# Two groups of heads side by side in a gated recurrence with a two-layer block behind it

## The chip, the cores and the metric

The kernel runs on one core of a Trainium2 chip. The metric is the device time of one execution in microseconds, taken over several runs of the same program. The engines are named as in the profile: PE multiplies matrices (PEld loads its weights), DVE and ACT and POOL work on vectors, SP only issues transfers. Each engine takes its instructions in the order in which they stand in its own queue and waits on semaphores for the others.

## What is computed

For each of 4 x 8 heads a 40 x 40 state runs through 768 time steps. The output of a step is read from the state as it was before the step.

```python
for t in range(S):
    y[:, :, t] = np.einsum('bhd,bhde->bhe', rt, state)
    Sa = np.einsum('bhde,bhe->bhd', state, at)
    state_decay = state * wt[:, :, None, :] - np.einsum('bhd,bhe->bhde', Sa, bt)
    state = state_decay + np.einsum('bhd,bhe->bhde', vt, kt)
...
x = y.transpose(0, 2, 1, 3).reshape(B * S, H * D)      # 3072 x 320
h = x @ w_in                                           # 320 x 2048
sp = np.maximum(h, 0.0) + np.log1p(np.exp(-np.abs(h)))
out = (h * erf(sp)) @ w_out                            # 2048 x 320
```

## The kernel before

**Tiling.** The 32 heads form 2 groups of 16. Time is cut into 6 segments of 128 steps, and a segment into 4 chunks of 32. So there are 2 x 6 = 12 segment steps (`q`) and 48 chunks. In a chunk the recurrence becomes products of small matrices; only the state, held in `MT` for one group, goes from a chunk to the next.

**Per segment step.** `prep` loads the decays `w` into a tile of the ring `Pr` and scans them forward and backward on DVE. `aphase`, once for each chunk, loads `k`, `b` and `a` (`kba`, into `bk`), scales them (`ab`, `bk`), multiplies them on PE (`A`, line 677) into the scores, masks them into a tile of the ring `Zs`, copies that tile's rows by transfers (`zs`, `AD`) and keeps the transposed keys in the ring `sg` (`bT`, line 695). `tphase` inverts the triangular score matrices of the four chunks: transfers `Ti`, `Ap`, 28 short DVE operations (`Tm`, `Ts`), transfers `TD` and `tb`, and two rounds of products on PE (`W` and `DAD`, line 740). The inverses lie in the ring `Tb`.

**The chain.** `chain`, once for each chunk, is the part that is serial: copy the state to `Zm` (`zmm`), `Z` on PE (line 785), copy `zt`, `U` on PE (line 794) with the inverse, copy `us`, from there four transfers `zu` into `Vu` and a transpose `UT` (line 821), copy `vtu`, `PQ` (line 830), mask `PQm`, and `MY` (lines 841 and 845), which gives the output of the chunk and the increment of the state. `MT` (line 848) adds it to the state, `Ym` (line 852) puts the output aside. `pmt` (line 812) transposes the state for `MY`. `v` and `r` come by the transfers `zv`, `vx`, `rt`, `rv`.

**The two-layer block.** When the four chunks of a segment are done, their 256 rows go to DRAM (`xw`) and come back transposed (`xr`, in `load_x`). `mm1` (line 1006, 192 in all, 8 matmuls each) makes `h`; `tanh`, `unit` and `post` form `h * erf(sp)` on ACT, DVE and POOL (`nd` line 1038, `rho` line 1039, `E` line 1050, `G` line 1051); `mm2` (line 1060) multiplies by `w_out`. At the start, `weights` turns both weight matrices from float64 to float32 with DVE, ACT and POOL work (`w1` to `w6`), after transfers `wd`.

**The order.** Every operation is recorded with its inputs, outputs and a priority. The instructions are then written out in the order of the table `ORDER`, on the engine that the string `ENGINES` names for each (P, A, V, G for POOL, S for SP). An entry -1 or -2 in `ORDER` is a filler: a 128x512 matmul on PE whose result nobody reads (`warm`, line 579). All transfers go through the helper `dma` (line 576), which issues on the engine that `ENGINES` names, SP or POOL. Here 493 transfers are recorded for SP and 414 for POOL, which also does 85 operations of vector work. All 24 chunks of group 0 come before those of group 1, and `mlp(q)` follows the chain of step `q`. The rings have 8 tiles `Zs`, 8 `sg`, 3 `Pr`, 2 `Tb`, 2 `Vu`, 2 `Rt`, 2 `vt` and 1 each of `Zm`, `Us`, `Sm` and `zt`; there is one state `MT`.

Of the kernel before, what the change touches and what calls it, by code (L numbers as in the profile page):

```python
# [1198 lines left out]
```

## Time and profile before

| | |
|---|---|
| median of 3 runs | 826.29 us (821.66, 826.29, 826.45) |
| profiled execution | 821.56 us, its span 819.8 us, so 1.8 us lie around the span |
| mean granted TensorE clock | 0.974 |
| busy in the span | PE 728.6, PEld 567.6, DVE 635.4, ACT 568.8, POOL 352.8 us |
| transfers | 98.98 MB, 49.95 MB in the queue of SP and 46.88 MB in that of POOL |

Busy time is an average over a start in which PE mostly waits, a long middle and an end. A row of the list of groups gives line, engine, operation, output and inputs, shapes and count; behind the first bar the busy time and the mean duration of one in ns; behind the second the idle time of the engine just before and what ended most of it. A row of the timeline gives start and duration in us. Where several matmuls stand in one row, their durations overlap, so the row's length and not the mean is what PE spent.

### The profile page before, as it was taken

The page shows a single profiled execution, that of the slowest core. Times are in us where ns is not written, and L with a number is a line of the kernel's source. Part 1 is how long each engine was busy: PE and PEld are TensorE (multiplying, and loading weights), DVE is VectorE, ACT ScalarE, POOL GpSimd, SP SyncE. Part 2 cuts the span into 40 slices and gives each one's busy share as a digit, 9 for nine tenths or more (in the row PEclk, how much of TensorE's full clock was granted, in tenths as well). Part 3 has the DMA queues.
Part 4 walks back from the last instruction along what each step waited for, and adds up shares of the span by engine and source line. Part 5 has one row for each costly group of instructions (what it writes and reads, how often), then busy time and mean ns, then how long its engine had stood idle before and what let it go on. Part 6 is the DMA issues. An engine that isn't in the chain of part 4 may idle for free.

```text
span 819.8 us, 32461 instructions
## 1 busy us (share of the span) xinstructions
PE 728.6 (89%) x13753; PEld 567.6 (69%) x13753; DVE 635.4 (78%) x1343; ACT 568.8 (69%) x1077; POOL 352.8 (43%) x503
## 2 busy tenths in 40 slices
...
GB/s 248 207 219 113 184 118 148 131 118 131 118 134 107 129 118 146 134 159 128 132 93 136 138 121 122 133 110 123 136 133 119 121 102 76 98 43 54 12 17 20
DMA packets 128728, 98.98 MB, mean 121 GB/s; under 512 B 88112, under 2 KB 111264, under 8 KB 128576
## 3 DMA queue, kind: packets, MB, share of 16 engines
q1 hardware_dynamic: 108144, 49.95, 25.5%
q0 software_dynamic: 20432, 46.88, 21.7%
q8 instruction: 110, 1.80, 0.9%
...
HBM read 75.07 MB, written 14.16 MB: 109 GB/s over the span
## 4 chain that ended last, share of the span: by engine, by line
PE 48%; DMA 15%; DVE 13%; ACT 10%; issue 8%; POOL 3%; SPq 2%; DVEq 0%; POOLq 0%; ACTq 0%
PE po L1060 17%; PE ph L1006 12%; DMA Vu<-Us 3%; PE pA L740 3%; PE my L841 3%; ACT r L1014 3%; ACT l L1014 2%; PE pA L677 2%; DMA Tb<-TD 2%; PE my L785 2%; PE my L794 2%; SPq L576 2%; DMA wo<-in_moe_w_in 2%; PE pQ L812 2%; PE pQ L830 2%
## 5 line engine op out<-in xcount | busy, mean ns | idle before, releaser
L1060 PE MATMUL po<-wo,h 128*128 128x320 f32 x768 | 250.7, 455 | 6.1 <-DVE h L1051 5.3
L1060 PEld LDWEIGHTS po<-wo,h 128*128 128x128 f32 x768 | 136.7, 195 | 49.0 <-DVE h L1051 7.0
L1014 ACT ACTIVATE l<-l 128x512 f32<-128x512 f32 x192 | 111.9, 626 | 10.7 <-DVE nd L1038 9.8
L576 POOL DMA_DIRECT2D Vu<-Us x88 | 49.5, 567 | 115.1 <-ACT Us L571 76.1
L1006 PE MATMUL ph<-xh,wih 128*128 128x256 f32 x384 | 97.5, 335 | 0.8 <-ACT h L571 0.8
L1006 PE MATMUL ph<-xl,wih 128*128 128x256 f32 x384 | 77.3, 283 | 0.0
L1006 PE MATMUL ph<-xh,wil 128*128 128x256 f32 x384 | 77.2, 283 | 0.0
L1051 DVE SCALAR_TENSOR_TENSOR h<-l,h 128x512 f32<-128x512 f32 x96 | 71.3, 748 | 2.2 <-POOL l L1050 1.4
L1039 DVE SCALAR_TENSOR_TENSOR r<-nd,r 128x512 f32<-128x512 f32 x96 | 67.9, 707 | 4.6 <-POOL nd L1038 2.8
L1006 PEld LDWEIGHTS ph<-xh,wih 128*128 128x128 f32 x384 | 61.9, 190 | 11.9 <-ACT h L571 1.6
L1038 DVE TENSOR_TENSOR nd<-l,r 128x512 f32<-128x512 f32 x80 | 57.4, 718 | 14.3 <-ACT r L1014 11.2
L841 PE MATMUL my<-Vu,sg 64*40 64x72 f32 x1536 | 49.4, 232 | 14.3 <-DMA Vu<-Us 5.2
L571 ACT COPY Zm<-MT 40x320 f32<-40x320 f32 x66 | 30.1, 456 | 45.0 <-DVE MT L848 41.8
L1006 PEld LDWEIGHTS ph<-xh,wil 128*128 128x128 f32 x384 | 59.8, 191 | 0.0
L1006 PEld LDWEIGHTS ph<-xl,wih 128*128 128x128 f32 x384 | 59.5, 191 | 0.0
L1014 ACT ACTIVATE l<-h 128x512 f32<-128x512 f32 x96 | 56.3, 627 | 3.9 <-DVE h L573 2.1
L571 ACT COPY h<-ph 128x512 f32<-128x512 f32 x82 | 47.1, 584 | 16.7 <-PE ph L1006 12.4
L579 PE MATMUL ph<-d 104*128 104x512 bf16 x216 | 57.5, 416 | 0.0
L841 PEld LDWEIGHTS my<-Vu,sg 64*40 64x40 f32 x1536 | 37.3, 115 | 28.3 <-issue 6.0
L1014 ACT ACTIVATE r<-r 128x512 f32<-128x512 f32 x96 | 55.0, 623 | 0.3
L1050 DVE TENSOR_TENSOR l<-l,r 128x512 f32<-128x512 f32 x75 | 52.1, 701 | 3.2 <-ACT l L1014 2.6
L1014 ACT ACTIVATE r<-l 128x512 f32<-128x512 f32 x96 | 54.5, 619 | 0.0
...
## 6 DMA issues: line engine op xcount, KB each, us to landing
...
```

Of the source, the lines that this page charges most:

```text
L571: self.nc.scalar.copy(o, i)
L576: self.P.add(name, "SP", lambda e: self.eng(e).dma_start(o(), i()), rd, wr, pr, ISSUE.get(name, 0.41))
L579: self.nc.tensor.matmul((self.ph[1], self.pQ)[x], self.d1[:, :128], self.d1[:, :512], start=True, stop=True)
L740: nc.tensor.matmul(pw[js, i], l[js, i], r[js, i], start=True, stop=True)
L841: nc.tensor.matmul(my[h * 64:h * 64 + 40, x, j], sg[xs, j, h], vu[xs, j // 2 * 2 + h, j % 2], start=True, stop=False)
L1006: nc.tensor.matmul(ph[:, j * 256:j * 256 + 256], a[:k, fs], b[:k], start=(m == 0), stop=(m == 7))
L1014: self.P.add(name, "ACT", lambda e: nc.scalar.activation(out=o, in_=i, **kw), rd, wr + ["act"], pr, 0.62)
L1038: P.add("nd", [("DVE", 0.69), ("POOL", 1.28)], lambda e, r=r, l=l, nd=nd: s.eng(e).tensor_tensor(out=nd, in0=l, in1=r, op=ALU.mult), [("l" ...
L1039: P.add("rho", "DVE", lambda e, r=r, nd=nd: nc.vector.scalar_tensor_tensor(out=r, in0=nd, scalar=2 * C4, in1=r, op0=ALU.add, op1=ALU.mult) ...
L1050: P.add("E", [("POOL", 1.28), ("DVE", 0.69)], lambda e: s.eng(e).tensor_tensor(out=l, in0=l, in1=r, op=ALU.mult), [("r", ir)], [("l", il)] ...
L1051: P.add("G", "DVE", lambda e: nc.vector.scalar_tensor_tensor(out=h, in0=l, scalar=-1.0, in1=h, op0=ALU.add, op1=ALU.mult), [("l", il)], [( ...
L1060: nc.tensor.matmul(po, h[:, bs], s.wo[:, f], start=(f == 0), stop=(f == 15))
```

## The change

The chunks of the two groups are put in one list of slots. Group 0 runs 6 chunks ahead (`glag=6`); then a chunk of group 0 and one of group 1 alternate, and the last 6 slots are group 1 alone. Segment steps are numbered by their first slot, and `mlp` of a step follows its last chunk. Each group has its own state tile, so the clearing between the groups (`MT0`) is gone. The rings grow: `Zs` and `sg` from 8 to 11, `Pr` from 3 to 4, `Tb` from 2 to 3. The scratch for POOL's transfers is cut from 16384 to 512 bytes, and in the new `ENGINES` no transfer is left on POOL: all 907 recorded transfers stand on SP. `ORDER` and `ENGINES` are new throughout.

```diff
+SCRATCH = 512
-SCRATCH = 16384
...
+def slots(lag):
+
+    a, b = [[(g, s_, c) for s_ in range(NS) for c in range(NC)] for g in range(2)]
+    o = []
+    for k in range(len(a) + lag):
+        o += a[k:k + 1] + (b[k - lag:k - lag + 1] if k >= lag else [])
+    return o
...
-        self.K = dict(zs=8, ab=1, p=3, sg=8, zm=1, vu=2, sm=1, rt=2, tb=2, us=1, ar=1, bk=2, vt=2, zt=1, tc=4, tg0=4, tg=0, tl=88, tmp=1, h=8, units=[4] * 24, l=6, r=4, n=1, xr=3, x=2, ob=1, wt=1)
+        self.K = dict(zs=11, ab=1, p=4, sg=11, zm=1, vu=2, sm=1, rt=2, tb=3, us=1, ar=1, bk=2, vt=2, zt=1, tc=4, tg0=4, tg=0, tl=88, tmp=1, h=8, units=[4] * 24, l=6, r=4, n=1, xr=3, x=2, ob=1, wt=1, glag=6)
...
-        s.MTp = s.sb.tile([104, NP // 2, 104], F32, name="MT")
-        s.MT = restride(s.MTp[:, :, 0:80].rearrange("p a (x e) -> p a x e", x=2), 2, 64)
+        s.MTp = ring("MT", NG, [104, NP // 2, 104])
+        s.MT = [restride(x[:, :, 0:80].rearrange("p a (x e) -> p a x e", x=2), 2, 64) for x in s.MTp]
...
-        if ck == 0 and g > 0:
-            P.add("MT0", [("POOL", 0.36), ("DVE", 0.33)], lambda e: s.eng(e).memset(MT, 0.0), (), ["MT"], pr)
...
+        for k, (g, s_, c) in enumerate(N.slots):
+            ahead(k)
+            q = N.Q[g, s_]
+            assert not any(y == q for y, _ in todo), (k, q, todo[:3])
             tag(q)
-            if check and q == nst - 1:
-                N.check(t(q, 3))
-            mlp(q)
+            N.chain(k, g, s_, c, t(k), t(k) + vlag, t(k) - tmargin)
+            if c == NC - 1:
+                if check and q == nst - 1:
+                    N.check(t(k))
+                mlp(q)
```

`ahead(k)` records `prep`, `aphase` and `tphase` of later steps as soon as the rings have a free tile. Of the vector work, 66 operations move from DVE to POOL (15 `E`, 12 `nd`, 12 `ab`, 17 `bk`, 7 `w5`, 2 `wlo`, 1 `MTs`), 11 `xl` move from POOL to DVE, and about 30 short copies out of PSUM move from ACT to DVE. PE has the same products as before, and 288 fillers where it had 216. Lines of the changed kernel stand 15 to 17 later: `Z` is line 800, `U` 809, `UT` 836, `PQ` 845, `MY` 856 and 860, `pmt` 827, `A` 694, `bT` 712, `mm1` 1021, `mm2` 1075, `dma` 592.

On PE, before, in the middle of the run (chunk 20; `Zm` and `Zs` go into `Z`, `zt` and `Tb` into `U`, `Us` into `UT`, `vt` into `PQ`, `Vu` and `sg` into `MY`):

```order
L785 MATMUL my_117<-Zm0_77,Zs4_72 32x40 x16
L794 MATMUL my_117<-zt0_109,Tb1_84 32x40 x16
L677 MATMUL pA_115<-Ab0_76,bk0_99 64x2x32 x8
L821 MATMUL pQ_116<-ident_112,Us0_85 80x128 x2
L1060 MATMUL po1_161<-wo_129,h_130 128x320 x3
L695 MATMUL pA_115<-ident_112,bk0_99 128x104 x4
L1060 MATMUL po0_160<-wo_129,h_130 128x320
L830 MATMUL pQ_116<-vt0_107 64x2x32 x8
L677 MATMUL pA_115<-Ab0_76,bk1_100 64x2x32 x8
L841 MATMUL my_117<-Vu0_78,sg4_95 40x72 x4
```

On PE, after, at a like place (slot 24; the `PQ` and the `MY` in these rows belong to the slot before, which is the other group's):

```order
L845 MATMUL pQ_125<-vt1_116 64x2x32 x8
L800 MATMUL my_126<-Zm0_80,Zs1_69 32x40 x16
L1075 MATMUL po1_170<-wo_138,h_139 128x320 x2
L1075 MATMUL po0_169<-wo_138,h_139 128x320 x2
L827 MATMUL pQ_125<-ident_121,MT0_118 104x104 x4
L1075 MATMUL po1_170<-wo_138,h_139 128x320
L809 MATMUL my_126<-zt0_117,Tb2_88 32x40 x16
L694 MATMUL pA_124<-Ab0_79,bk0_107 64x2x32 x8
L856 MATMUL my_126<-Vu1_82,sg2_98 40x72 x4
```

Before, `U` stands directly behind `Z`, and all steps of one chunk follow each other with a few products between; after, other products stand between `Z` and `U`, and the `MY` of one group stands behind the `Z` and `U` of the other.

On SP, before, in the middle of the run, the four `zu` of one chunk (`Vu` from `Us`) stand in one piece:

```order
L576 DMA Rt1_82<-in_r_e 104x256
L576 DMA Ap_102<-AD0_118 64x16x32
L576 DMA Vu0_78<-Us0_85 32x4x40 x4
L576 DMA Zs3_71<-Ab0_76 40x2x128
L576 DMA Zm0_77<-in_v_s 32x640
```

On POOL, before, a little later, the transfers of an inversion (`TD` out to DRAM, `Tb` back):

```order
L576 DMA Vu0_78<-Us0_85 32x4x40 x2
L576 DMA Vu1_79<-in_v_x 32x8x40
L576 DMA bk1_100<-in_kba_e 104x1024
L576 DMA TD1_121<-Ti_101 64x512 x2
L576 DMA Zs7_75<-Ab0_76 40x2x128
L576 DMA Tb1_84<-TD1_121 64x16x32 x2
```

On SP, after, slot 25, where the third and the fourth `zu` of a chunk are the first and the last of these rows:

```order
L592 DMA Vu1_82<-Us0_89 32x4x40
L592 DMA Tb1_87<-TD1_130 64x16x32 x2
L592 DMA Zm0_80<-in_v_s 32x640
L592 DMA Ap_110<-AD1_128 64x16x32
L592 DMA Vu0_81<-in_v_x 32x8x40
L592 DMA Zs9_77<-Ab0_79 40x2x128
L592 DMA Pr1_92<-in_w_e 104x1033
L592 DMA vt0_115<-in_rv_e 80x8x96
L592 DMA vt1_116<-in_rv_e 80x8x96
L592 DMA Zs10_78<-Ab0_79 40x2x128
L592 DMA Vu1_82<-Us0_89 32x4x40
```

What stood on two queues stands on one: the transfers of an inversion and the loads for later chunks are now between the `zu` of one chunk.

More of the change, by code (lines that the diff above doesn't have):

```diff
@@ new lines @@
+    "VAAAGAGSVVAAAVAGSVVAAAVAVSVVAAAVAVSVVAAAVAVSVVAAAVAGSVVAAAVAVSVVAAAGAAVAVSVVAAAVAAVAGSVVAAAGSVVAAAGSVVAAAGSVVAAAGSVVAAAGSVVAAAGSVVAAAVSVVAAA"
+    "GSVVAAAVSVVAAAGSAVVAVSGSSGPVVSSPASVSSGPVVSSPVSGSSVPVVSSPASGSSVPVVSSPVSSSSAAVVVVVVVVVVVVVVVVVVVVVVVVVVVVSSSSVPPPPVPPPPVSAVVVVSGSSGPVVSSPASVSS"
+    "GPVVSSPVSVSSVPVVSSPASSSSSVVPVPVVVAAPAPAPVPVVSVSSGPVVSSPVSSSSAAVVVVVVVVVVVVVVVVVVVVVVVVVVVVSSSSVPPPPVPPPPVSAVVAVSSSSSAAPAPVAVAAPAPAPVPVVSVSSG"
+    "PVVSSPVSSSSSVAPAPAAAAAPAPAPVPVVSGSSGPVVSSPVSSSSSAVPAPAAAAAPAPAPVPVVSSSSSVVSAVSSAVPPVAPPVAPPVAPPAAAAAAAAAAAAAAAAGVVVGVVVAAAAAPPAAPPAAVVPPPPPP"
@@ new lines @@
+    "AAGVPPPPPPAAGVPPPPGVPPPPSVSSVPVVSSPASSSSSVVAPAPASSSSPAPVPVPVVSVSSGPVVSSPASSSSAAVVVVVVVVVVVVVVVVVVVVVVVVVVVVSSSSVPPPPVPPPPVSAVVVVSSSSSAVPAPVS"
+    "SSSPAPVPVPVVSGSSVPVVSSPVSSSSSAAPAPVSSSSPAPAPVPVVSGSSGPVVSSPASSSSSAAPVPVSSSSPVPAPVPVVSSSSSAVPAPASSSSPVPAPVPVVSSSSSAVSAVSSAVAAAAAAAAAAAAAAGVVV"
+    "GVGVAAAAAPPAAPPAAGVPPPPPPAAGVPPPPPPAAGVPPPPVVPPPPVSASAAAAAAAAAAAAAAVVVVGVVVAAAAAPPVAPPAAVVPPPPPPAAGVPPPPPPAAGVPPPPGVPPPPSVSSGPVVSSPASGSSGPVV"
+    "SSPVSSSSAAVVVVVVVVVVVVVVVVVVVVVVVVVVVVSSSSVPPPPVPPPPVSAVVAVSSSSSAAPAPASSSSPAPAPVPVVSVSSGPVVSSPVSSSSSVAAPVPASSSSPAPAPVPVVSSSSSVVPAPASSSSPVPVP"
@@ L233 @@
+    "VVVGVAAAAAPPAAPPVAVVPPPPPPAAGVPPPPPPAAGVPPPPVVPPPPSSSSSVAVPVPVSSSSPAPVPVPVVSSSSSAAPAPASSSSPAPVPVPVVSSSSSVAPVPVSSSSPVPVPVPVVSSSSSVAPAPASSSSPV"
+    "PAPVPVVSSSSVPVVSVGSVVSSVGAAAAAAAAAAAAAAVVVVVVVVAAAAAPPAAPPAAVVPPPPPPAAVVPPPPPPVAGVPPPPVVPPPPVSVSAAAAAAAAAAAAAAVVVVVVVVAAAAAPPVAPPAAVVPPPPPPA"
+    "AVVPPPPPPVAGVPPPPGVPPPPAAAAAAAAAAAAAAVVVVVVVVAAAAAVVPPPPVVPPPPVVPPPPVVPPPPASAS"
 )
-SCRATCH = 16384
 PARAMS = dict(K=dict(warm=43.6))
@@ L497, in __init__ @@
         self.tc, self.nc, self.I, self.out = tc, tc.nc, I, out
-        self.K = dict(zs=8, ab=1, p=3, sg=8, zm=1, vu=2, sm=1, rt=2, tb=2, us=1, ar=1, bk=2, vt=2, zt=1, tc=4, tg0=4, tg=0, tl=88, tmp=1, h=8, units=[4] * 24, l=6, r=4, n=1, xr=3, x=2, ob=1, wt=1)
+        self.K = dict(zs=11, ab=1, p=4, sg=11, zm=1, vu=2, sm=1, rt=2, tb=3, us=1, ar=1, bk=2, vt=2, zt=1, tc=4, tg0=4, tg=0, tl=88, tmp=1, h=8, units=[4] * 24, l=6, r=4, n=1, xr=3, x=2, ob=1, wt=1, glag=6)
         self.K.update(K)
         K = self.K
+        self.slots = slots(K["glag"])
+        self.steps = list(dict.fromkeys((g, s_) for g, s_, c in self.slots))
+        self.Q = {x: q for q, x in enumerate(self.steps)}
+        self.nz = {}
         self.P = Plan(K.get("po", {}), self.warm, K.get("warm", 4.0), order=ORDER, engines=ENGINES)
@@ L612, in start @@
             ms("zmy", s.my[:, x], 0.0, ["my", "pz"], (("DVE", 0.6),))
-        ms("zMT", s.MTp, 0.0, ["MT"])
+        for g in range(NG):
+            ms("zMT", s.MTp[g], 0.0, [("MT", g)])
         for j in range(len(s.XL)):
@@ L646, in aphase @@
         s, nc, P = self, self.nc, self.P
-        q, ck = g * NS + s_, s_ * NC + c
-        n = q * NC + c
+        q, ck = s.Q[g, s_], s_ * NC + c
+        n = s.nz[g, s_, c] = len(s.nz)
         Wt, Pf = s.WT[q % len(s.WT)], s.PR[q % len(s.PR)]
@@ L747, in tphase, with chain @@
         P.add("Tb", "DVE", lambda e: nc.vector.tensor_tensor(out=tb, in0=pw, in1=tb, op=ALU.add), ["pA"], ktb, pr, 0.67)
-    def chain(self, g, s_, c, pr, prl, prt):
+    def chain(self, n, g, s_, c, pr, prl, prt):
         s, nc, P, K = self, self.nc, self.P, self.K
         I = s.I
-        q, ck = g * NS + s_, s_ * NC + c
-        n = q * NC + c
+        q, ck = s.Q[g, s_], s_ * NC + c
         ip = q % len(s.PR)
@@ L757, in chain @@
         ix = lambda R: n % len(R)
-        iz, im, ig, iv, ism, irt, iu, ivt, izt = map(ix, (s.ZS, s.ZM, s.SG, s.VU, s.SM, s.RT, s.US, s.VT, s.ZT))
+        im, iv, ism, irt, iu, ivt, izt = map(ix, (s.ZM, s.VU, s.SM, s.RT, s.US, s.VT, s.ZT))
+        iz, ig = (s.nz[g, s_, c] % len(R) for R in (s.ZS, s.SG))
         zs, zm, sg, vu, sm, rt, us, zt = s.ZS[iz], s.ZM[im], s.SG[ig], s.VU[iv], s.SM[ism], s.RT[irt], s.US[iu], s.ZT[izt]
         tc = K["tc"]
-        it = n // tc % len(s.TB)
+        it = q % len(s.TB)
         tb = s.TB[it][:, c % tc]
@@ L771, in chain @@
         s.dma("rv", lambda: vr[:, :, :96], lambda: I["rv_e"][g, ck].rearrange("p (a x) -> p a x", a=NP), wr=[("vt", ivt, 0), ("vt", ivt, 1)], pr=prl)
-        if ck == 0 and g > 0:
-            P.add("MT0", [("POOL", 0.36), ("DVE", 0.33)], lambda e: s.eng(e).memset(MT, 0.0), (), ["MT"], pr)
-        elif c == 0 and ck > 0:
-            P.add("MTs", [("POOL", 0.8), ("DVE", 0.49)], lambda e: s.eng(e).tensor_tensor(out=MT, in0=MT, in1=P3[:, :, L:L + 1].rearrange("p (a x) e -> p a x e", x=2).to_broadcast([104, NP // 2, 2, 40]), op=ALU.mult), [("p", ip)], ["MT"], pr)
+        if c == 0 and ck > 0:
+            P.add("MTs", [("POOL", 0.8), ("DVE", 0.49)], lambda e: s.eng(e).tensor_tensor(out=MT, in0=MT, in1=P3[:, :, L:L + 1].rearrange("p (a x) e -> p a x e", x=2).to_broadcast([104, NP // 2, 2, 40]), op=ALU.mult), [("p", ip)], [kM], pr)
         for h in range(2):
-            P.add("zmm", [("ACT", 0.43), ("DVE", 0.32)], lambda e, h=h: s.copy(e, zm[0:40, :, h].rearrange("p (a x) e -> p a x e", x=2), MT[h * 64:h * 64 + 40]), ["MT"], [("zm", im, "m", h)], pr)
+            P.add("zmm", [("ACT", 0.43), ("DVE", 0.32)], lambda e, h=h: s.copy(e, zm[0:40, :, h].rearrange("p (a x) e -> p a x e", x=2), MT[h * 64:h * 64 + 40]), [kM], [("zm", im, "m", h)], pr)
         pz = s.my[:, 0, 320:480].rearrange("p (q e) -> p q e", q=NQ)
@@ L811, in mmt @@
             for i in range(NP // 2):
-                nc.tensor.transpose(pt[:, i], s.MTp[:, i], s.ident[:104, :104])
-        P.add("pmt", "PE", mmt, ["MT", "ident"], ["pQ", "pQb"], pr, 0.4)
+                nc.tensor.transpose(pt[:, i], MTp[:, i], s.ident[:104, :104])
+        P.add("pmt", "PE", mmt, [kM, "ident"], ["pQ", "pQb"], pr, 0.4)
         P.add("ysM", [("ACT", 0.43), ("DVE", 0.48)], lambda e: s.copy(e, sm, restride(pt[:, :, 0:80].rearrange("p a (h e) -> p a h e", h=2), 2, 64)), ["pQ", "pQb"], [("sm", ism)], pr)
@@ L847, in chain @@
         P.add("MY", "PE", mmy, [("sg", ig), ("sm", ism), ("rt", irt), ("vu", iv, "v", 0), ("vu", iv, "v", 1), ("vu", iv, "p")] + [("vu", iv, "u", j) for j in range(4)], ["my"], pr, 0.95)
-        P.add("MT", "DVE", lambda e: nc.vector.tensor_tensor(out=MT, in0=MT, in1=my[:, :, :, 0:40].rearrange("p x j e -> p j x e"), op=ALU.add), ["my"], ["MT"], pr, 0.49)
+        P.add("MT", "DVE", lambda e: nc.vector.tensor_tensor(out=MT, in0=MT, in1=my[:, :, :, 0:40].rearrange("p x j e -> p j x e"), op=ALU.add), ["my"], [kM], pr, 0.49)
         py = my[:, :, :, 40:72].rearrange("p x j t -> p j x t")
@@ L1077, in build @@
         nst = NG * NS
-        t = lambda q, c: t0 + (4 * q + c) * D
-        m = lambda u: t0 + 4 * D + Dm * u + lag
+        at = {}
+        for k, (g, s_, c) in enumerate(N.slots):
+            at[g, s_, c] = k
+        t = lambda k: t0 + k * D
+        done = [at[g, s_, NC - 1] for g, s_ in N.steps]
+        m = lambda u: t(done[min(int(u / 2), nst - 1)] + 1) + Dm * (u - 2 * min(int(u / 2), nst - 1)) + lag
+        pq = lambda q: t(at[N.steps[q] + (0,)]) - amargin
         def prep(q):
-            N.prep(q // NS, q % NS, t(q, 0) - amargin)
+            N.prep(*N.steps[q], pq(q))
         def aph(q, c):
-            N.aphase(q // NS, q % NS, c, t(q, 0) - amargin + 3 * c)
+            N.aphase(*N.steps[q], c, pq(q) + 3 * c)
         def tph(q):
-            N.tphase(q // NS, q % NS, t(q, 0) - amargin + 15)
+            N.tphase(*N.steps[q], pq(q) + 15)
         sizes, nb = N.K["units"], 8 * nst
```

108 lines of the change are left out of this document (48 added, 60 removed), and 363 rows, old and new, of the table ORDER.

## The prediction

> **What bounds the kernel now.** I read the page first, then windows that cut the span where the work changes, then the timeline of PE at the start, then the groups of the chain.
>
> ```profile
> PE 728.6 (89%) x13753; PEld 567.6 (69%) x13753; DVE 635.4 (78%) x1343; ACT 568.8 (69%) x1077; POOL 352.8 (43%) x503
> PE 48%; DMA 15%; DVE 13%; ACT 10%; issue 8%; POOL 3%; SPq 2%; DVEq 0%; POOLq 0%; ACTq 0%
> ```
>
> PE is the busiest engine, but only half of the chain that ended last runs through it. The cuts are the first `mm1` (135.3 us) and the end of the last `MY` (750.7 us); the last row is the fillers (line 579) alone, in the first stretch.
>
> ```profile
> 0.00:135.30 135.30, 94.05 (x1610) 53.69 (x1610) 99.23 (x216) 64.50 (x138) 53.94 (x79) 0.92 0.68 178
> 135.30:750.70 615.40, 577.04 (x11858) 470.29 (x11859) 494.90 (x1061) 454.66 (x860) 293.56 (x420) 0.99 0.48 119
> 750.70:819.80 69.10, 57.50 (x306) 43.61 (x295) 41.28 (x67) 49.60 (x80) 5.26 (x5) 0.94 0.08 24
> ...
> 0.00:135.30 135.30, 57.51 (x216) 21.22 (x216) 0.92 0.68 178
> ```
>
> The columns after the length are busy PE, PEld, DVE, ACT, POOL, then the clock. The start has 94.05 - 57.51 = 36.5 us of useful PE work in 135.3 us. The middle is PE's: 577.0 of 615.4 us, so **38.4 us idle** in it, 0.87 us for each of its 44 chunks. The end has one last segment to push through the block, 69.1 us. So the change can win in the start, and at most 38 us in the middle, unless it shortens busy PE, for which these rows show no way.
>
> What is the idle time behind? The products of the chain and of the inverse, and `mm2`:
>
> ```profile
> L841 PE MATMUL my<-Vu,sg 64*40 64x72 f32 x1536 | 49.4, 232 | 14.3 <-DMA Vu<-Us 5.2 <-DMA vt<-in_rv_e 2.8 <-DVE Vu L833 2.6
> L785 PE MATMUL my<-Zm,Zs 96*32 96x40 f32 x1536 | 25.1, 211 | 4.4 <-DMA Zm<-in_v_s 2.9 <-DVE Zm L573 1.3
> L794 PE MATMUL my<-zt,Tb 32*32 32x40 f32 x1536 | 24.2, 202 | 4.5 <-ACT zt L571 1.9 <-issue 1.7 <-DVE zt L573 0.4
> L740 PE MATMUL pA<-Tb,T 32*32 32x32 f32 x1536 | 18.0, 197 | 5.6 <-issue 3.9 <-DVE T L744 1.6
> L740 PE MATMUL pA<-T,Ap 32*32 32x32 f32 x1536 | 17.4, 200 | 10.6 <-issue 5.2 <-DVE T L733 3.6 <-DMA Ap<-AD 1.6
> L1060 PE MATMUL po<-wo,h 128*128 128x320 f32 x768 | 250.7, 455 | 6.1 <-DVE h L1051 5.3
> ```
>
> `MY`, `Z` and `U` sit idle 23.2 us in the span, a few of them in the start; the inverse 16.2 us, about half in the start; `mm2` 6.1. I put the middle's 38.4 us at 22 for the chain, 8 for the inverse and 8 for the rest.
>
> **The change, term by term, against the profiled execution** (span 819.8 us, 821.6 with what lies around it; the median of the runs, 826.3, is 4.7 higher).
>
> *Start.* PE's timeline before:
>
> ```profile
> 25.98 1.12 PE L677 MATMUL pA<-Ab,Pr 104*64 104x64 f32 x16 [0.82 <-POOL Ab L667]
> 30.24 0.96 PE L695 MATMUL pA<-ident,Pr 104*128 104x104 f32 x4 [3.13 <-DVE Zs L684]
> ...
> 35.44 25.19 PE L579 MATMUL ph<-d 104*128 104x512 bf16 x106
> 63.87 1.93 PE L740 MATMUL pA<-T,Ap 32*32 32x32 f32 x128 [3.24 <-issue]
> ...
> 115.58 0.28 PE L845 MATMUL my<-Rt,Sm 40*40 40x32 f32 x8
> ...
> 121.37 1.79 PE L740 MATMUL pA<-T,Ap 32*32 32x32 f32 x128 [1.91 <-DVE T L733]
> ...
> 125.48 1.60 PE L740 MATMUL pA<-Tb,T 32*32 32x32 f32 x101 [1.63 <-DVE T L744]
> ...
> 130.20 1.12 PE L677 MATMUL pA<-Ab,bk 104*64 104x64 f32 x16
> ...
> 135.31 0.51 PE L1006 MATMUL ph<-xh,wih 128*128 128x256 f32 x2
> ```
>
> A filler costs 25.19 / 106 = 0.238 us. The new order has 174 of them ahead of the first `W` instead of 106: 40 after the third `A` (the row at 25.98) and 134 more behind the fourth `bT`. If the third `A` still ends at 27.1, the first `W` can't start before 27.1 + 174 x 0.238 + two `bT` and one `A` (3.0) = 71.5, which is **7.6 later** than 63.87. SP's new order also puts `wd13`, `wd14` and `wd17` ahead of the first `TD`, so the transfers may not allow it earlier anyway. From there to the end of the fourth `MY` (115.9) it was 52.0 us; between the first and the fourth `MY` the order now has 45 fillers for 69, 24 x 0.238 = 5.7 us less, and I take 46. From the fourth `MY` to the first `mm1` it was 19.4 us, with the second step's `W`, `DAD`, two `A` and more ahead of `mm1`. Now only 48 fillers, `pmt` and `Z` stand there, 48 x 0.238 + 1.3 = 12.7 us. The data need `Ym`, four `xw`, their landing, four `xr` and theirs:
>
> ```profile
> L576 SPq DMA_DIRECT2D xd<-Pr x33: 309/353/1090, 116.4 to 753.2; - x33
> xd<-Pr POOLq DMA_DIRECT2D x15, 80.0 KB, 3.2
> xr<-xd POOLq DMA_DIRECT2D x11, 128.0 KB, 3.6
> L576 SPq DMA_DIRECT2D xr<-xd x27: 395/635/1308, 178.5 to 757.9; - x27
> ```
>
> That is 4 x 0.353 + 3.2 + 4 x 0.635 + 3.6 = 10.8 us, some 13 with `Ym`, `xh` and `xl`; POOL's landings stand for SP's, which the trace doesn't give. I take 13.5. First `mm1` at 71.5 + 46 + 13.5 = **131**. Ends: 122 if the chain's 52 us shrink to the quickest of its chunks, 143 if none of the fillers saved shows and SP's one queue delays the inverse.
>
> *Middle.* PE's work is 577.0 us plus what no longer precedes `mm1`: `W` 1.79, `DAD` about 2.2, an `A` 1.12, and a second `A`, a `bT`, `U`, `UT` and `PQ`, none above 1.12: 8 us together, so 585. For the idle time I counted, in both orders, what PE has to do between dependent products of chunks 8 to 43, at this trace's durations: between `Z` and `U` 1.3 us on average before, 3.9 after; `U` to `UT` 1.7 and 3.6; `PQ` to `MY` 1.6 and 3.6; from `MY` to the next `Z` of the same group 4.0 and 8.4. The inverse has no more room (`W` to `DAD` about 2.2 in both). So I let the chain's 22 us shrink to 4 and leave 8 + 8: idle **20**. Ends: 8, and 45 when SP's queue costs a few waits. Middle 605.
>
> *One queue for all transfers.* This is what may eat the gain. SP's time for one issue (min/median/max, ns):
>
> ```profile
> L576 SPq DMA_DIRECT2D Vu<-Us x88: 585/612/1644, 132.4 to 744.2; - x88
> L576 SPq DMA_DIRECT2D Zs<-Ab x56: 779/842/1274, 15.7 to 726.9; - x56
> L576 SPq DMA_DIRECT2D AD<-Zs x55: 303/434/1293, 25.6 to 669.6; - x55
> L576 SPq DMA_DIRECT2D Vu<-in_v_x x52: 569/614/1006, 73.6 to 744.8; - x52
> L576 SPq DMA_DIRECT2D Rt<-in_r_e x30: 321/508/1468, 107.1 to 729.3; - x30
> L576 SPq DMA_DIRECT2D Zm<-in_v_s x27: 320/414/1382, 87.8 to 677.5; - x27
> L576 SPq DMA_DIRECT2D vt<-in_rv_e x24: 585/610/1488, 91.4 to 726.2; - x24
> L576 SPq DMA_DIRECT2D bk<-in_kba_e x15: 324/503/1271, 2.6 to 621.5; - x15
> ```
>
> A chunk needs 4 x 0.612 + 2 x 0.842 + 2 x 0.434 + 2 x 0.614 + 0.508 + 0.414 + 0.610 + 0.503 = 8.3 us, and a quarter of the step's 19 transfers (between 0.353 and 0.65 each, say 0.5) 2.4: **10.7 us** of 13.7 us (605 / 44). Behind a waiting transfer all others wait, the `zu` of the other group too, and PE's `MY` waits for these. The order puts 4.5 us of issues between the first and the end of the fourth `zu` of a chunk, on average, where SP had 1.5. I cost this at nothing, since a group now has two slots, 27 us, for what took one; the cover is gone in the first and last six slots, where one group runs alone.
>
> On this the Trainium skill, in "DMA: Bandwidth & Descriptors", section "Issuing engines are not separate DMA queues", says that issuing from several engines only saves the sequencer's time to start a transfer, usually small beside the transfer. By that rule the sum stays as it is and the rival on SP below has no price. Here an issue of `zu` is 0.612 us; small it isn't when 10.7 of 13.7 us are issues.
>
> *Vector engines.* 66 operations go to POOL. Before, DVE's busy share in the middle is 80%, and it loses more than it gets, so I give this no term. *End.* 18 `mm1` and 64 `mm2` remain behind the last `MY`, as against 18 and 66, and ACT and PE do there what they did: **69**.
>
> Sum: 131 + 605 + 69 = 805, and 1.8 around it: **806 us**.
>
> **Rivals.**
>
> *The slack isn't the limit.* `Zm`, `Us`, `Sm` and `zt` still have one tile each, so a slot of one group waits for the other's copies and transfers, and the chunks march as before though the order alternates them. For it: PE's idle time is spread over many releasers, none large. Against: the gaps on PE have doubled. The middle keeps its 38.4: 131 + 585 + 38 + 69 + 1.8 = 825.
>
> *SP becomes the bound, slower.* Waits of today's SP queue (total, times, longest):
>
> ```profile
> SPq L576 <- PE my L845: 54.5, 15, 15.1
> SPq L576 <- DVE Pr L852: 38.0, 13, 7.5
> ```
>
> SP has 13.7 - 10.7 = 3.0 us for waits in each chunk; from there on it decides. With one wait for `MY` (54.5 / 15 = 3.6 us) in each chunk and one for `Ym` (2.9) in each step, a chunk takes 10.7 + 3.6 + 0.7 = 15.0 us, the middle 44 x 15.0 = 660, and the whole 131 + 660 + 69 + 1.8 = 862. Against: the same waits were harmless with SP at 40%, and an order can put a transfer behind its cause.
>
> *POOL holds up DVE, slower.* One place of this trace:
>
> ```profile
> 628.44 1.31 POOL L1050 TENSOR_TENSOR l<-l,r 128x512 f32<-128x512 f32 x1
> ...
> 628.08 2.23 DVE L1051 SCALAR_TENSOR_TENSOR h<-l,h 128x512 f32<-128x512 f32 x1
> ...
> L1050 DVE TENSOR_TENSOR l<-l,r 128x512 f32<-128x512 f32 x75 | 52.1, 701 | 3.2 <-ACT l L1014 2.6
> L1050 POOL TENSOR_TENSOR l<-l,r 128x512 f32<-128x512 f32 x21 | 28.3, 1349 | 31.5 <-ACT l L1014 25.2 <-DVE r L1039 6.0
> ```
>
> A DVE operation with two inputs took 2.23 us beside POOL's, 0.7 without. If each moved operation blocks DVE, it takes 1.35 us of it instead of 0.70: 66 x 0.65 = 43 us, and if PE waited for all of it, 806 + 43 = 849. For: that row. Against: with 21 of these on POOL already, the mean of DVE's 75 is 701 ns, so such pairs seldom meet. The Trainium skill, "SBUF — State Buffer", section "Who interferes with whom", says just this, that a DVE instruction with two SBUF inputs contends with a GpSimd instruction that reads SBUF; the trace agrees.
>
> **How the numbers follow.** A difference under 1% (818 to 834.6 around the median of 826.3) couldn't be told from none. The forecast, 790 to 822, has 0.53; no gain in the middle, 825, 0.20; SP as the bound, 840 upward, 0.19; POOL and DVE, 835 to 849, 0.08. Faster takes nearly all of the first and a bit of the second; a part of POOL's case falls within 1%. The range 786 to 850 leaves out most of SP's case and the best start with the least idle time.
>
> **What the profile after would show.** The first `W` near 71, the first `mm1` near 131 (start); PE idle near 20 us between there and the last `MY` (middle), with `MY`'s wait for `Vu` smaller; SP's waits; the mean of DVE's `G` (line 1051) no higher than 0.75 us. I am wrong if `MY` waits longer for `zu`, which is SP's case, or if the inverse of the first step comes after 80 us.

## The result, and the profile after

The changed kernel takes **858.34 us** (median of four runs) against 826.37 us (821.66 to 832.60) of the kernel before: ratio **1.034** (95% interval 1.025 to 1.044), slower. One of the four runs, at 1730.21 us, was disturbed; the median counts it and the ratio leaves it out (the others took 849.49, 857.55 and 859.12 us, 855.4 in the mean). The forecast was 806, the range 786 to 850.

The profiled execution took 849.49 us, so it is the quickest of them; its span is 847.7 us. First its page: the engines, the one queue that is left, and the chain that ended last.

```profile
PE 748.0 (88%) x13825; PEld 580.9 (69%) x13825; DVE 628.4 (74%) x1314; ACT 564.3 (67%) x1051; POOL 183.9 (22%) x147
...
q1 hardware_dynamic: 211308, 96.81, 48.3%
...
PE 46%; DVE 18%; DMA 11%; SPq 9%; ACT 6%; issue 6%; POOL 1%; DVEq 0%; ACTq 0%; POOLq 0%
```

POOL lost half of its busy time: the time of its 414 issues is gone, and the 66 added vector operations take less. DVE hardly got shorter. SP's issues have risen from 2% to 9% of the chain, DMA fell from 15% to 11%, DVE rose from 13% to 18%. The same cuts as before, at the first `mm1` (now 127.3) and the end of the last `MY` (780.9); columns as before.

```profile
0.00:127.30 127.30, 96.86 (x1338) 52.50 (x1339) 96.85 (x201) 62.37 (x128) 33.98 (x31) 0.97 0.68 178
127.30:780.90 653.60, 596.54 (x12218) 486.21 (x12216) 492.30 (x1051) 453.28 (x847) 144.13 (x111) 0.97 0.50 114
780.90:847.70 66.80, 54.56 (x277) 42.16 (x272) 39.21 (x63) 48.70 (x78) 5.79 (x5) 0.95 0.08 25
```

And PE's timeline at the start, the same places as before (start, length):

```profile
44.44 29.09 PE L595 MATMUL ph<-d 104*128 104x512 bf16 x134
74.18 1.43 PE L757 MATMUL pA<-T,Ap 32*32 32x32 f32 x128 [0.65 <-issue]
...
115.52 0.25 PE L860 MATMUL my<-Rt,Sm 40*40 40x32 f32 x8
...
127.31 0.59 PE L1021 MATMUL ph<-xh,wih 128*128 128x256 f32 x2
```

The start is 8.0 us shorter and the end 2.3 us. The middle is **38.2 us longer**: PE is busy 596.5 us for 577.0, and idle 57.1 us for 38.4. Everything that went wrong is in the middle, so the next cut is there. Of the kernel before, and then of the kernel after, the middle's first 200 us and the rest:

```profile
140.00:340.00 200.00, 182.37 (x3839) 148.72 (x3840) 161.92 (x358) 144.51 (x277) 104.78 (x150) 0.98 0.52 126
340.00:740.00 400.00, 379.67 (x7744) 308.92 (x7743) 322.32 (x684) 300.62 (x567) 183.22 (x262) 0.99 0.47 117
```

```profile
140.00:340.00 200.00, 170.48 (x3569) 138.03 (x3569) 149.87 (x329) 123.12 (x236) 51.65 (x40) 0.93 0.53 122
340.00:740.00 400.00, 374.81 (x7611) 306.37 (x7610) 312.96 (x669) 297.14 (x555) 75.62 (x58) 0.98 0.51 116
```

From 140 to 340 us PE is idle 29.5 us for 17.6 and its clock is 0.93 for 0.98; in the 400 us behind, 25.2 for 20.3. Two thirds of the extra idle time and most of the loss of clock are in the first stretch.

### The profile page after: what moved, and what is told of

Read it like the earlier page. It is cut to its first block, busy times and chain, and to the rows that moved or that the text cites. A ratio compares the mean times of both kernels' runs of the same rounds, so it can differ in the third digit from the quotient of the medians.

```text
span 847.7 us, 32375 instructions
## 1 busy us (share of the span) xinstructions
PE 748.0 (88%) x13825; PEld 580.9 (69%) x13825; DVE 628.4 (74%) x1314; ACT 564.3 (67%) x1051; POOL 183.9 (22%) x147
## 2 busy tenths in 40 slices
DMA packets 211459, 98.96 MB, mean 117 GB/s; under 512 B 165132, under 2 KB 198668, under 8 KB 211308
## 3 DMA queue, kind: packets, MB, share of 16 engines
q1 hardware_dynamic: 211308, 96.81, 48.3%
## 4 chain that ended last, share of the span: by engine, by line
PE 46%; DVE 18%; DMA 11%; SPq 9%; ACT 6%; issue 6%; POOL 1%; DVEq 0%; ACTq 0%; POOLq 0%
PE po L1075 13%; PE ph L1021 12%; SPq L592 9%; PE my L856 3%; PE pA L757 3%; DMA Tb<-TD 3%; PE pA L694 3%; PE pQ L845 2%; PE ph L595 2%; ACT r L1029 2%; PE pA L712 2%; DVE Zs L701 2%; DVE h L1066 2%; DVE r L1054 2%; PE my L809 2%
## 5 line engine op out<-in xcount | busy, mean ns | idle before, releaser
L1065 POOL TENSOR_TENSOR l<-l,r 128x512 f32<-128x512 f32 x36 | 50.9, 1418 | 151.0 <-DVE r L1054 61.5
L1066 DVE SCALAR_TENSOR_TENSOR h<-l,h 128x512 f32<-128x512 f32 x96 | 73.1, 770 | 0.6
L595 PE MATMUL ph<-d 104*128 104x512 bf16 x288 | 69.9, 393 | 0.0
L587 ACT COPY h<-ph 128x512 f32<-128x512 f32 x77 | 44.7, 580 | 32.2 <-PE ph L1021 27.3
L856 PE MATMUL my<-Vu,sg 64*40 64x72 f32 x1536 | 51.1, 238 | 14.2 <-ACT Us L587 4.3
L684 POOL TENSOR_TENSOR Ab<-bk,Pr 104x512 f32<-104x512 f32 x20 | 25.4, 1269 | 160.8 <-DMA Zs<-Ab 69.2
L1053 DVE TENSOR_TENSOR nd<-l,r 128x512 f32<-128x512 f32 x68 | 49.6, 729 | 14.0 <-ACT r L1029 11.6
L1053 POOL TENSOR_TENSOR nd<-l,r 128x512 f32<-128x512 f32 x28 | 37.7, 1346 | 102.1 <-ACT r L1029 49.4
```

Source lines behind the costliest of these rows:

```text
L587: self.nc.scalar.copy(o, i)
L595: self.nc.tensor.matmul((self.ph[1], self.pQ)[x], self.d1[:, :128], self.d1[:, :512], start=True, stop=True)
L856: nc.tensor.matmul(my[h * 64:h * 64 + 40, x, j], sg[xs, j, h], vu[xs, j // 2 * 2 + h, j % 2], start=True, stop=False)
L1053: P.add("nd", [("DVE", 0.69), ("POOL", 1.28)], lambda e, r=r, l=l, nd=nd: s.eng(e).tensor_tensor(out=nd, in0=l, in1=r, op=ALU.mult), [("l" ...
L1065: P.add("E", [("POOL", 1.28), ("DVE", 0.69)], lambda e: s.eng(e).tensor_tensor(out=l, in0=l, in1=r, op=ALU.mult), [("r", ir)], [("l", il)] ...
L1066: P.add("G", "DVE", lambda e: nc.vector.scalar_tensor_tensor(out=h, in0=l, scalar=-1.0, in1=h, op0=ALU.add, op1=ALU.mult), [("l", il)], [( ...
```

## The experiments

Times are medians; the ratios are to the kernel before, run beside each. The kernel after has 1.034, so a run at 1.016 has won back 1.8 points, of 8.3 us each. The interval of 1.034 reaches 0.9 points to each side, and every such difference has at least that uncertainty.

### One queue on the old order

```diff
- engine of a recorded transfer: as the table has it (493 SP, 414 POOL)
+ engine of a recorded transfer: SP
```

> The kernel before with its own order on every engine, but all its transfers issued by SP; nothing else differs. If the loss comes from the one queue alone (theory A), it shows here too: 845 to 862 us, with more DMA packets as after. If it comes from the new order, side by side (theory B), this stays near 826, 818 to 835. If POOL's moved vector operations cost it (theory C), also near 826 or below.

1004.97 us, ratio **1.225** (1.217 to 1.233), far beyond what theory A expected. PE's longest sum of waits, and a piece of the chain that ended last (start, length, what):

```profile
PE my L841 <- DMA Vu<-Us: 76.1, 30, 6.5
```

```profile
401.64 0.50 SPq L576
...
406.56 0.67 SPq L576
...
407.28 5.27 DMA Zm<-in_v_s
...
412.68 0.49 PE my L785 x29
```

`MY` waited 5.2 us for `zu` before and 76.1 here. In the piece SP issues one transfer behind the other for 5.6 us, the last of them is `zv`, and `Z` waits for it. The second dose, half of the moved transfers:

```diff
- engine of POOL's transfers: POOL
+ engine of POOL's transfers: SP for every second one of each name (212 of 414)
```

> The kernel before in its own order with every second of POOL's transfers given to SP, 212 of 414 moved, by name. If SP's load decides only above a threshold (the prediction put it at 3.0 us of waits in a chunk, which 705 of 907 transfers would leave at about 5.4), little shows: 826 to 850. If every moved transfer costs alike, half of the 180 us: 905 to 925.

941.25 us, ratio **1.140** (1.133 to 1.147): 115 us for 212 transfers, 0.54 us each, and 183 us for 414, 0.44 each. Neither expectation is met. At half the dose, which by the same count left SP some 5.4 us for waits in a chunk, SP's load is not free: on an order made for two queues each moved transfer costs about as much as its issue takes. Smaller doses were not run. With one queue the newly searched order takes 147 us less than the old one; how much of the loss that is left is still the one queue's, these two runs don't say.

### Is it still SP in the kernel after?

```diff
+LEAVE, KEEP = ("zv", "vx", "rt", "rv"), 4
 for i in order:
+    if o["name"] in LEAVE and seen[o["name"]] > KEEP: continue
     o["fn"](o["eng"])
```

> The kernel after, without the five loads zv, vx (two), rt and rv of a chunk after the first few chunks, so that later chunks compute with old inputs (the output is not the reference's): some 220 of 907 issues less on SP, 2.8 us of 10.7 us per chunk. A: SP is the bound, so the time falls by 25 us or more, to 833 or less. B: no more than 5 us. C: no change.

832.96 us, ratio 1.016 (1.011 to 1.020). That looks like A, and it is why the control matters: the same cut in the kernel before.

> The control of the run with fewer loads: the kernel before, two queues, without zv, vx, rt and rv after the first few chunks (it computes with old inputs; the output is not the reference's). If those 25 us were the one queue's (A), two queues have little to gain here: 818 to 826. If loads and their bytes cost in any kernel (D), this falls by 15 us or more too, to 811 or less.

809.79 us, ratio 0.979 (0.974 to 0.984). The cut gives 1.9 points after and 2.1 points before, the same within the intervals. What these loads cost, they cost in both. The first 200 us of the middle, after, then before, both with the cut:

```profile
140.00:340.00 200.00, 174.44 (x3740) 141.31 (x3738) 153.76 (x340) 128.63 (x247) 52.12 (x40) 0.94 0.42 96
340.00:740.00 400.00, 381.60 (x7813) 312.59 (x7806) 321.15 (x681) 305.50 (x569) 80.45 (x62) 1.00 0.34 79
```

```profile
140.00:340.00 200.00, 189.83 (x3954) 155.32 (x3951) 165.16 (x366) 149.83 (x285) 88.03 (x120) 0.97 0.37 92
340.00:740.00 400.00, 381.12 (x7735) 309.27 (x7734) 321.95 (x685) 301.59 (x569) 149.81 (x206) 0.98 0.32 80
```

Idle 25.6 against 10.2 in the first stretch, 18.4 against 18.9 behind it: with SP relieved, *all* of the extra idle time is in the first 200 us. Next, shorter issues, and both cuts together:

```diff
+THIN = dict(zu=16, vx=4, zs=24)
-    self.eng(e).dma_start(o(), i())
+    y, x = (o(), i()) if the count is below THIN[name] else one of 4 to 8 blocks of each
+    self.eng(e).dma_start(y, x)
```

> The kernel after, with every transfer, wait and place on SP kept, but zu, vx and zs cut to a fraction of their rows after the first chunks (old data in the rest; the output is not the reference's), so that SP needs less time for each of these 364 issues: if 0.3 us are left of 0.61 (zu, vx) and 0.84 (zs), 120 us less, as much as the 224 left out. A, SP's time to issue is what counts: 828 to 845. If what counts is that a waiting transfer holds up those behind it (G): 850 to 862, since no wait is gone.

841.30 us, ratio 1.017 (1.012 to 1.023), but the premise failed. SP's issues in this kernel (min/median/max, ns):

```profile
L602 SPq DMA_DIRECT2D Vu<-Us x176: 507/582/1655, 144.5 to 769.0; - x176
L602 SPq DMA_DIRECT2D Vu<-in_v_x x96: 311/471/1552, 18.0 to 753.7; - x96
```

Cut to a quarter, `zu` still takes 0.58 us for 0.61, and `zs` 0.79 for 0.84; `vx`, cut to an eighth, falls from 0.61 to 0.47. The sum is some 23 us shorter, not 120. The gain of 1.7 points is then as likely that of the smaller transfers; between A and G this decides nothing.

> Both cuts together in the kernel after: no zv, vx, rt, rv after the first chunks, and short zu and zs, so SP's issues fall from some 585 us to 370 or less. If the order side by side does give the chain the slack of the prediction and SP hides it, PE's idle time in the middle falls from 57 to about 20 to 30 us and the time to 800 to 815. If the order has no such slack (B), idle time stays above 40 and the time at 825 to 835.

835.84 us, ratio 1.011 (1.007 to 1.016). Idle time in the first 200 us is 25.7 us, as with the loads alone:

```profile
140.00:340.00 200.00, 174.33 (x3625) 141.73 (x3626) 155.29 (x340) 126.15 (x242) 51.48 (x40) 0.92 0.38 87
```

B's expectation holds, but for 0.8 us in the time: idle time in the middle is 46.7 us. With this much taken off SP no hidden slack appears. SP still issues 683 transfers there, for 493 in the kernel before, so the one queue isn't cleared altogether.

### Other queues, without a new order

```diff
- engine of zv, vx, rt (rv): SP
+ engine of zv, vx, rt: POOL        (first run)
+ engine of zu: POOL for every second one     (second run)
+ engine of zv, vx, rt, rv: ACT     (third run)
```

> The kernel after, in its own order, with zv, vx (two) and rt of a chunk issued by POOL instead of SP, 180 issues of 907; rv stays on SP. Nothing is left out, so the bytes moved stay. If SP's time to issue is the bound (A), taking 180 x 0.54 = 97 us of issues off it gives most of the 25 us that 224 issues gave: 835 to 845. If the transferred bytes or the DMA engines' queue were what the shortened kernel gained by (D), this stays at 852 to 862.

888.54 us, ratio 1.074 (1.065 to 1.083).

> The kernel after with every second of the four zu transfers of a chunk issued by POOL instead of SP, 88 of 176; the order is unchanged. A: the four zu no longer queue on SP and SP has 1.2 us less per chunk, so the time falls to 835 to 850. B: stays within 5 us of 858. C: slower, since POOL has more to issue.

855.47 us, ratio 1.039 (1.034 to 1.044), no change, as B says; `zu` lands there after 2.5 us from POOL (2.3 before).

> The kernel after, in its own order, with the 224 issues of zv, vx, rt and rv on ACT's queue instead of SP's. A: as with POOL, 833 to 845, less what ACT pays: 224 issues of some 0.55 us are 123 us of ACT's time, beside 564 busy, so it may eat the gain (855 to 880). D: 855 or more.

920.87 us, ratio 1.115 (1.107 to 1.123). A missed the first and the third. D missed the first; its "855 or more" covers the third, but it has no reason for a loss of 62 us. POOL's longest wait for a buffer in the first:

```profile
POOL Zm L592 <- PE my L800: 44.3, 14, 9.9
```

A load whose buffer isn't free yet makes POOL wait, 44.3 us for `Z` to release `Zm` alone, and POOL's `E`, `nd` and `ab` stand behind it; on ACT its activations do. That this is what made both runs slower is how I read it: such an issue needs a queue in which nothing urgent stands behind it, which is a matter of the order.

### POOL's vector operations

```diff
- E, nd, bk, ab, w5, wlo on POOL: 125
+ 65 of these on DVE, evenly along the program
```

> The kernel after with 65 of the vector operations that went to POOL (E, nd, bk, ab, w5, wlo) given back to DVE, evenly along the program, in the same order. C: POOL held up DVE or PE waited for POOL's longer operations, so the time falls by 10 us or more, to 848 or less. A and B: within 5 us of 858, or slower, since DVE gets 46 us more work.

863.47 us, ratio 1.047 (1.041 to 1.053): not faster, so theory C falls. `G`'s mean duration is 770 ns after, 748 before, and 728 with these operations back on DVE. If the neighbours on POOL make the difference, they cost `G` 42 ns each, 4 us of DVE in all.

### Side by side with one planner

```diff
-ORDER, ENGINES = (...), (...)
+ORDER, ENGINES = (), ""       # the program's own list planner makes the order
-glag=6
+glag=24                       # the second run only
```

> The code after with its two tables emptied, so that its own list planner makes the order from the same costs; the second group six slots behind; all transfers on SP. It is to be set beside the next run. Side by side is worth something in itself (E): at least 15 us less than the next run. It is worth nothing (F): within 8 us of it. Absolute time: 850 to 920.

> The same, with the lag at 24 slots, so that the second group starts when the first has ended: one change, no other. E: at least 15 us slower than side by side. F: within 8 us. If one queue for all transfers is what costs and side by side hides it, it stands with E, and here some 30 to 100 us slower, since on the order before one queue cost 180 us.

1076.45 us (1.305, 1.295 to 1.316) and 1158.09 us (1.404, 1.395 to 1.414). E holds: from the same code and the same planner, the groups side by side take 82 us less. The planner chooses order and engines anew for each, so the lag isn't quite the only difference. These orders are far worse than the searched ones, PE idle 167 and 209 us in the middle, so there were waits to fill; in the kernel before 38 were left.

### Shared tiles, vector work, close products

```diff
-zm=1, sm=1, us=1, zt=1
+zm=2, sm=2, us=2, zt=2
-s.wil = [... for k in range(2)]
+s.wil = [s.mb.tile([128, 2048], F32R, name="wil0")] * 2
```

> The kernel after, same order, with two tiles each of Zm, Us, Sm and zt instead of one, so that one group's slot doesn't wait for the other's readers; room for them comes from wil1 put on wil0 (one product of mm1 takes the wrong weights; the output is not the reference's). If the shared tiles are what keeps the chunks marching as before (H, a rival of the prediction): idle time in the middle falls by 15 us or more and the time to 835 or less. If not: within 6 us of 858.

851.64 us, ratio 1.033 (1.025 to 1.041).

> The same with two tiles, and without zv, vx, rt and rv after the first chunks. H, the tiles being hidden behind SP's load: 815 or less, where fewer loads alone gave 833. Not H: 827 to 837.

837.16 us, ratio 1.015 (1.008 to 1.023). With 1.033 for 1.034 and 1.015 for 1.016, H falls twice; the first 200 us are idle 28.1 us in the first of them. One tile that both groups share stayed single here, `my`, which `Z`, `U` and `MY` write (see below).

```diff
+LEAVE, KEEP = ("E", "nd"), 4
```

> The kernel after, all transfers kept, without the vector products E and nd (188 of the 192 left out, of them 62 on POOL and some 126 on DVE; the block computes with the wrong values). If PE's idle time is the order's waiting for vector results (V): it falls from 57 to 45 or less and the time by 18 us or more, to 840 or less, and by at least 10 us more than the same cut gives the kernel before. If vector work isn't it: within 6 us of 858.

845.17 us, ratio 1.026 (1.018 to 1.034).

> The control: the kernel before without E and nd after the first four of each (188 left out). V: no more than 8 us faster than 826. If every kernel gains by it: 810 or less.

815.28 us, ratio 0.988 (0.984 to 0.992): 0.9 points after, 1.2 points before. Both times lie between the two values expected, but V's condition fails: the cut gives no more after than before. DVE has a tenth to a fifth less to do in the two stretches (135.5 us for 149.9, 251.3 for 313.0), and PE's idle time after stays as it was, 29.9 and 26.4:

```profile
140.00:340.00 200.00, 170.14 (x3583) 138.19 (x3582) 135.52 (x320) 124.46 (x240) 27.96 (x23) 0.93 0.54 123
```

```diff
- ORDER: ..., U, UT, mm2, ...
+ ORDER: ..., U, mm2, UT, ...   (28 such moves on PE after, 39 before)
```

> The kernel after with 28 instructions of PE's block (mm1, mm2 and a few others) pulled forward by some places, each between two dependent products that stood too close for what lies between them (copies, transfers); other engines' order unchanged. By the durations of the trace this takes 10.7 us of 27.5 us that such places are short by. If the short places make the idle time (W): it falls from 57 to about 47 and the time by 8 to 15 us, to 843 to 850. If the waits come from SP and the vector queues, late whatever PE does: within 4 us of 858.

> The kernel before, treated alike: 39 of PE's instructions pulled forward, 12.8 us of 31.1 us that its close places are short by, most of it ahead of MY. W: 8 to 15 us faster than 826, which would beat both kernels. Otherwise within 4 us of 826.

859.98 us (1.038, 1.034 to 1.043) and 826.60 us (1.001, 0.997 to 1.005). W falls: idle time in the middle is 65 us after, and before it goes from 38 to 34 with no gain in time. No version that leaves nothing out is faster than the kernel before.

### What is left: does PE lack work of the block?

Cuts in SP's load and in the vector work give after what they give before, and these and the second tiles leave 25 to 30 us of idle time between 140 and 340 us. So I read what PE has to do there. `mm1`'s first matmul, before, in four stretches (count: durations, first and last start):

```profile
L1006 PE MATMUL ph<-xh,wih x14: 279/284/387, 152.8 to 167.7; 128*128 128x256 f32 x14
...
L1006 PE MATMUL ph<-xh,wih x10: 280/283/388, 189.9 to 199.5; 128*128 128x256 f32 x10
...
L1006 PE MATMUL ph<-xh,wih x4: 282/284/384, 235.9 to 237.0; 128*128 128x256 f32 x4
...
L1006 PE MATMUL ph<-xh,wih x8: 278/283/522, 257.4 to 261.4; 128*128 128x256 f32 x8
```

and after:

```profile
L1021 PE MATMUL ph<-xh,wih x14: 280/365/562, 154.0 to 172.2; 128*128 128x256 f32 x14
...
L1021 PE MATMUL ph<-xh,wih x8: 279/283/525, 218.7 to 221.9; 128*128 128x256 f32 x8
...
L1021 PE MATMUL ph<-xh,wih x26: 280/283/882, 221.8 to 255.5; 128*128 128x256 f32 x26
...
L1021 PE MATMUL ph<-xh,wih x16: 280/283/386, 290.4 to 300.0; 128*128 128x256 f32 x16
```

The pauses are between segment steps: 22 and 20 us before, **47 and 35 us** after. A step's `mm1` needs its four chunks. One group after the other, the steps end with slots 3, 7, 11, 15, 19; with the second group six slots behind they end with slots 3, 8, 13, 16, 21. The second step starts on `mm1` 29 us later (218.7 for 189.9), the third 33 us (290.4 for 257.4). Only a part of this is the numbering: `MY` of slot 8 ends at 208.9 us after and at 193.9 before, so the chain is 15 us late there as well. From 140 to 340 us PE did 151 matmuls of `mm2` for 176, and 86 of this form of `mm1` for 112. A step has 64 of the one and 32 of the other, so PE is 0.4 and 0.8 of a step behind. How it looks without `mm1` to put in between, at the third inverse after (group 1's first):

```profile
181.68 1.17 PE L757 MATMUL pA<-T,Ap 32*32 32x32 f32 x114 [0.80 <-DVE T L750]
184.26 0.32 PE L757 MATMUL pA<-T,Ap 32*32 32x32 f32 x14 [1.41 <-issue]
185.38 1.61 PE L757 MATMUL pA<-Tb,T 32*32 32x32 f32 x114 [0.80 <-DVE T L761]
188.36 0.43 PE L757 MATMUL pA<-Tb,T 32*32 32x32 f32 x14 [1.37 <-issue]
189.59 0.76 PE L809 MATMUL my<-zt,Tb 32*32 32x40 f32 x32 [0.80 <-DVE Tb L764]
```

5.2 us idle in 8.7, with no work of the block between `W`, `DAD` and `U`. But there was such work: by 186.6 us `G` of the first step had ended four times, for eight matmuls of `mm2` each, and only 12 of these 32 had run. The other 20 stand behind `U` in the order. And PE is idle beside `mm1` too. The two pauses, before and then after:

```profile
168.70:189.90 21.20, 16.76 (x488) 12.35 (x488) 14.97 (x26) 14.19 (x27) 11.97 (x17) 1.00 0.44 102
...
238.00:257.40 19.40, 17.42 (x441) 12.02 (x439) 14.67 (x29) 13.15 (x26) 6.68 (x10) 0.91 0.57 136
```

```profile
173.20:218.70 45.50, 37.04 (x859) 27.21 (x857) 32.34 (x62) 25.78 (x51) 18.16 (x13) 0.89 0.47 110
...
256.50:290.40 33.90, 29.54 (x653) 20.99 (x650) 25.52 (x63) 22.31 (x46) 8.76 (x9) 0.95 0.43 105
```

In the pauses PE is idle 6.4 of 40.6 us before and 12.8 of 79.4 after, 16% both times. In the rest of the 200 us it is idle 11.2 of 159.4 us before (7%) and 16.7 of 120.6 after (14%). At the shares of before, the longer pauses would add some 3 us, an estimate, of the 11.9 that are new in these 200 us. So late steps can be a part of the loss, but not most of it. No run changes the lag under an order of equal quality, so no experiment shows even that part. How the 30 us between the two kernels divide between the late steps, the one queue and the waits of the next section stays open.

## Why the prediction was wrong

*Start, 131.* Right in kind: the first `W` at 74.2 (71.5 forecast), the fourth `MY` done at 115.8 (117.5), the first `mm1` at 127.3.

*End, 69.* 66.8.

*Middle, 605.* It failed here, 653.6: idle 57.1 for 20, and 11.5 more of busy PE. The step that failed is "I let the chain's 22 us shrink to 4": I counted PE's work between dependent products of one group, found it doubled on average, and made a gain of it. `MY`, `Z` and `U` in the middle, before and then after (the idle time ahead of them stands behind the second bar):

```profile
L841 PE MATMUL my<-Vu,sg 64*40 64x72 f32 x1404 | 45.6, 232 | 14.2 <-DMA Vu<-Us 5.2 <-DMA vt<-in_rv_e 2.8 <-DVE Vu L833 2.6
...
L785 PE MATMUL my<-Zm,Zs 96*32 96x40 f32 x1376 | 21.8, 207 | 1.4 <-DVE Zm L573 1.3
L794 PE MATMUL my<-zt,Tb 32*32 32x40 f32 x1376 | 21.5, 200 | 3.5 <-issue 1.7 <-ACT zt L571 0.9 <-DVE zt L573 0.4
```

```profile
L856 PE MATMUL my<-Vu,sg 64*40 64x72 f32 x1408 | 47.3, 239 | 13.3 <-ACT Us L587 4.3 <-DMA Vu<-Us 3.3 <-DVE Us L589 2.4
...
L809 PE MATMUL my<-zt,Tb 32*32 32x40 f32 x1408 | 22.4, 204 | 4.8 <-ACT zt L587 1.4 <-DVE Pr L867 1.2 <-DVE Tb L764 1.0
L800 PE MATMUL my<-Zm,Zs 96*32 96x40 f32 x1376 | 22.3, 208 | 3.1 <-ACT Zm L587 2.5 <-DVE Zm L589 0.2 <-ACT h L587 0.2
```

The three are idle 19.1 us before (I had put them at 22) and 21.2 after; they did not shrink to 4. That is 17 of the 37 us by which my idle time was too small. The two terms that I left at 8 us grew as well: the inverse has 12.8 us (8.2 before), the rest 23.1 (11.1 before).

What the distance was to cover did get shorter: `MY`'s waits for `zu` fell from 5.2 to 3.3 us, those for `rv` from 2.8 to none, those for the mask (`DVE Vu`) from 2.6 to 1.2. But `MY` has new waits, which the kernel before hasn't at all: 6.7 us for the copy `us` and 1.4 for the copy `zt`. One of them (start, length; idle before and its releaser in brackets):

```profile
249.70 0.49 PE L809 MATMUL my<-zt,Tb 32*32 32x40 f32 x32
...
250.30 0.29 ACT L587 COPY Us<-my 128x160 f32<-128x160 f32 x1 [2.59 <-DMA bk<-in_kba_e]
...
250.64 0.48 PE L856 MATMUL my<-Vu,sg 64*40 64x72 f32 x8 [0.46 <-ACT Us L587]
```

`Z`, `U` and `MY` of both groups write one tile, `my`. Side by side, the `U` of one group stands ahead of the other group's `MY`, and `MY` starts 0.05 us after the copy `us` has read that `U` out of `my`. In the run with two tiles of `Us` and `zt` such waits are still 5.1 us. Why it waits, though `U` fills other columns of the tile than `MY`, these rows don't say. So the order lengthened the distances inside a group and at the same time made one group wait for the other's copies, which my count of PE's work left out. No run gives `Z` and `U` a tile of their own, so what these 8.1 us are worth isn't shown by an experiment.

*The 8 us moved behind `mm1`.* Counted as PE work, which they are. But the second step's inverse was part of it, and the chunks behind it came later: five `MY` were done at 140 us before, four at 150 after. The start's gain was given back at once.

*The clock.* I had no term for it. By the same instructions PE's busy time in the middle is longer in the runs in which it waits more. The middles of the run with fewer loads and of the run with loads on ACT:

```profile
126.80:760.30 633.50, 585.22 (x12219) 477.42 (x12218) 491.39 (x1051) 452.54 (x848) 144.05 (x111) 0.98 0.36 83
```

```profile
126.30:853.00 726.70, 626.94 (x12219) 509.60 (x12218) 491.75 (x1052) 454.99 (x850) 140.70 (x111) 0.91 0.45 103
```

With 48.3 us idle PE is busy 585.2 us, with 99.8 us idle 626.9. Between these two runs a us of waiting went with 0.8 us more of busy time. Other runs scatter by several us: at 61.9 us idle PE is busy 605.8 us with the 65 operations back on DVE and 596.4 with half of `zu` on POOL.

*SP becomes the bound, 862.* The time came out near it, but the sign that I named for it didn't: `MY` waits less for `zu`, not longer. On the old order its threshold of 3.0 us a chunk is wrong by the half dose (1.140), and relieving SP after gives no more than before. SP's issues are 9% of the chain that ended last, for 2%, so a part of the loss may still be its. By the Trainium skill, "DMA: Bandwidth & Descriptors", section "Issuing engines are not separate DMA queues", what several issuing engines save is usually small beside the transfer; by that rule one queue should have cost little. The runs disagree, 1005 us for 822 on the same order.

*The slack isn't the limit, 825.* Its first half held: the chain's idle time stayed. Its single tiles are not the cause, since two of each change nothing; the copies that `MY` waits for come out of another shared tile, `my`. Its middle, with 38 us idle, was too short as well.

*POOL holds up DVE, 849.* Its sign came, `G` at 0.770 us where I named 0.75 as the limit, but not its price: giving operations back to DVE gains nothing, and leaving out `E` and `nd` gains no more than in the kernel before. The rule of the Trainium skill, "SBUF — State Buffer", section "Who interferes with whom", can account for 42 ns of a `G` here.
